# VectorE's frequency-domain sum written k1 by k1 into a tile of its own, one GpSimd sum behind it

## The chip, the cores and the metric

One core of one Trainium2 chip. The metric is the device time of one execution in microseconds, lower is better. The engines are named as in the profile: PE (TensorE matmul) and PEld (its weight load), DVE (VectorE), ACT (ScalarE), POOL (GpSimd) and SP (SyncE, which issues DMAs).

## The reference, cut to what matters

```python
u = x * v                                     # 4 batches, 11456 positions, 128 channels
h_filt = (np.maximum(pos_emb @ w1, 0) @ w2) * np.exp(-0.01 * pos)[:, None]
Uf = np.fft.rfft(u, n=2 * S, axis=1)
Hf = np.fft.rfft(h_filt, n=2 * S, axis=0)
y = np.fft.irfft(Uf * Hf[None], n=2 * S, axis=1)[:, :S]
attn = x * y
# then a mixture of experts on the 45824 rows of attn: top expert of 8 by
# logits = rows @ w_gate + modality_bias, out = gate * (relu(rows @ w1[e]) @ w2[e])
```

The change touches the product `Uf * Hf`, a complex multiplication for every batch, channel and frequency.

## The kernel before, in words

The convolution is a two-step transform by matmuls. The sequence is cut into N1 = 90 by N2 = 64; an outer transform over N1 turns positions n1 into k1, and a middle stage works on each k1: twiddle and transform over N2, multiply by the filter's spectrum, transform back. The kernel runs: filter, middle of batch 0, outer of batch 0 and 1, middle of batch 1, and so on, four middle stages in all; then the experts, which fill the second half of the execution. While a middle stage or outer stage of batch b runs, rows of batch b-1 are already sent to their expert's region by indirect DMAs that POOL issues (`send_rows`, L263).

A middle stage (`middle_stages`) walks over NG = 30 groups of G = 3 values of k1. Each group passes through stages that are shifted against each other by a table of steps (`MID`): in a step PE does, for four different groups, `turn` (six transposes to `aT`), `inverse` (twelve matmuls to `pw`), `back` (six transposes of the product to `yT`) and `spectrum` (twelve matmuls to `pz`). The order of PE, ACT, DVE and SP is the order of the program text, run step by step; each engine runs its own queue in order and waits for others by semaphores. POOL's order is that of the text too, with a `NoSync` dependency that puts one `send_rows` behind the second sum.

In `spectrum` of a group, `pz` in PSUM holds for both blocks (b) a real-like and an imaginary-like part (c) of 3 x 64 values with j, the k1 within the group, as the fastest index. The elementwise work on it is, in program order:

- L623 DVE twice: `more`[0], `more`[1] = parts of block 0 times a second filter row (128x384 each),
- L626: `more`[0] += `more`[1], on DVE for the first two groups of a stage (g < GD = 2), on POOL after that,
- L628 DVE twice: `part`[0], `part`[1] = all parts times the filter (128x768 each),
- L632 DVE: `part`[0] += `part`[1] (128x768, all of it in SBUF, in place),
- L633, on DVE or POOL like L626: block 1 of `part`[0] += `more`[0] (128x384),
- for g > 2 in batches 1 to 3, one L263 on POOL behind L633.

The result `part`[0] keeps j fastest, so `back` (L600 by way of the helper `turned`) transposes views with a step of three elements: `k["p"] = p.rearrange("p b c (k j) -> p b j (c k)", j=G)`. For block 0 the view is complete after L632, for block 1 after L633.

The tiles `aT`, `yT`, `part`, `more` and, in the outer stages, `seq`, `y` and `lT` come from one pool of NA = 11 buffers that are handed out in turn (`new_a`): a new tile waits until the tile that was handed out eleven requests ago has been read for the last time. `rings` holds the filter and twiddle constants, loaded ahead by SP.

Of the kernel before, what the change touches and what calls it, by code (L numbers as in the profile page):

```python
# [36 lines left out]
G = 3  # L37
# [139 lines left out]
def hyena_moe_kernel(ctx: ExitStack, tc: tile.TileContext, a: dict, out: bass.AP,  # L177
                     nb: int = B, nt: int = NF + NH):
    nc = tc.nc
    pe, act, dve, pool, sp = nc.tensor, nc.scalar, nc.vector, nc.gpsimd, nc.sync  # L180
# [13 lines left out]
    def bank(name):  # L194
        return banks[-1].tile([D, 512], F32, tag="ps", name=name)
# [30 lines left out]
    def ins_of(x):  # L226
        return getattr(x, "ins", x)
# [21 lines left out]
    def fetch(b):  # L249

        sp.dma_start(to_t[b % 2], xi[b].rearrange("(p c) -> p c", p=D))
        rows_back(b, 0)
        waiting.extend((b, c) for c in range(NR // D))

    def send_rows(n, behind=None, wait=None):


        for _ in range(min(n, len(waiting))):
            b, c = waiting.pop(0)
            if c % RC == 0:  # L260
                rows_back(b, c // RC + 1)
            ix, src = to_t[b % 2][:, c:c + 1], back_t[(b * NB + c // RC) % 3][:, c % RC]
            s = pool.indirect_dma_start(  # L263
                out=xs, out_offset=bass.IndirectOffsetOnAxis(ap=ix, axis=0), in_=src,
                in_offset=None, bounds_check=E * R - 1, oob_is_err=False)
            free_rows(scatters, s)
            if behind is not None:
                tc.add_manual_dep(ins_of(s), behind.name, order_dep, reason="order of issue")
            if wait is not None:
                tc.add_manual_dep(ins_of(s), wait.name, sync_dep, reason="pace")  # L270
# [83 lines left out]
    with ExitStack() as cv:  # L354
# [4 lines left out]
        GK = G * N2  # L359

        def pair(name):
            return pairs.tile([D, 2, 512], F32, tag="pp", name=name)

        def new_a(name, dt=F32):
            return st.tile([D, 1024], dt, tag="a", name=name, bufs=NA)
# [50 lines left out]
        def ring(name):  # L416
            r = ring_of[name]
            r[1] += 1
            return r[0][(r[1] - 1) % len(r[0])]
# [95 lines left out]
        def turn_back(g, blk, j):  # L515

            return A[:, blk, G * g + j].rearrange("p c n -> p (c n)")
# [53 lines left out]
        def middle_stages(b):  # L571

            kept = {}

            def load(g):
                k = kept[g] = {"b": ring("b")[0:2 * N2].rearrange("p (j d) -> p j d", j=G)}
                sp.dma_start(k["b"],
                             a["c_bc"][g, :, 0:2 * GK].rearrange("p (j d) -> p j d", j=G))
                h = k["h"] = ring("h").rearrange("p (m c k) -> p m c k", m=2, c=3)
                sp.dma_start(h[:, :, 1:3].rearrange("p m c k -> p m (c k)"),  # L580
                             hs[g].rearrange("p (m k) -> p m k", m=2))

            def minus(g):

                h = kept[g]["h"]
                act.mul(h[:, :, 0], h[:, :, 2], -1.0)

            def load_c(g):
                k = kept[g]
                k["c"] = ring("c")[0:2 * N2].rearrange("p (j d) -> p j d", j=G)  # L590
                sp.dma_start(k["c"],
                             a["c_bc"][g, :, 2 * GK:4 * GK].rearrange("p (j d) -> p j d", j=G))

            def turned(name, of):

                t = new_a(name)[0:2 * N2, 0:2 * G * D].rearrange("p (b m) -> p b m", b=2)
                for blk in range(2):
                    p = bank(name)
                    for j in range(G):
                        pe.transpose(p[0:2 * N2, D * j:D * j + D], of(blk, j), ident)  # L600
                    act.copy(t[:, blk], p[0:2 * N2, 0:G * D])
                return t

            def turn(g):
                kept[g]["aT"] = turned("aT", lambda blk, j: turn_back(g, blk, j))

            def spectrum(g):
                k = kept[g]
                pz = pair("pz")
                zv = pz[:, :, 0:2 * GK].rearrange("p b (m j) -> p b m j", j=G)  # L610
                for blk in range(2):
                    for j in range(G):
                        pe.matmul(zv[:, blk, :, j], k["aT"][:, blk, D * j:D * j + D],  # L613
                                  k["b"][:, j, :], start=True, stop=True)
                z = pz[:, :, 0:2 * GK].rearrange("p b (c m) -> p b c m", c=2)
                h = k["h"]


                part = [new_a("part")[:, 0:4 * GK].rearrange("p (b c m) -> p b c m", b=2, c=2)
                        for _ in range(2)]  # L620
                more = new_a("more")[:, 0:4 * GK].rearrange("p (b c m) -> p b c m", b=2, c=2)
                for i in range(2):
                    dve.tensor_mul(more[:, i], z[:, 0, i:i + 1].broadcast_to([D, 2, GK]),  # L623
                                   h[:, 1, 1 - i:3 - i])
                eng = dve if g < GD else pool
                eng.tensor_add(more[:, 0], more[:, 0], more[:, 1])  # L626
                for i in range(2):
                    dve.tensor_mul(  # L628
                        part[i], z[:, :, i:i + 1].broadcast_to([D, 2, 2, GK]),
                        h[:, 0:1, 1 - i:3 - i].broadcast_to([D, 2, 2, GK]))  # L630
                p = part[0]
                dve.tensor_add(p, p, part[1])  # L632
                added[0] = ins_of(eng.tensor_add(p[:, 1], p[:, 1], more[:, 0]))  # L633
                if g == GD and b > 0:
                    fetch(b - 1)
                if g > GD:
                    send_rows(1, added[0])
                k["p"] = p.rearrange("p b c (k j) -> p b j (c k)", j=G)

            def back(g):  # L640
                k = kept[g]
                k["yT"] = turned("yT", lambda blk, j: k["p"][:, blk, j])

            def inverse(g):
                k = kept.pop(g)
                for blk in range(2):
                    pw = bank("pw")
                    for j in range(G):
                        pe.matmul(pw[:, 2 * N2 * j:2 * N2 * (j + 1)],  # L649
                                  k["yT"][:, blk, D * j:D * j + D], k["c"][:, j, :],  # L650
                                  start=True, stop=True)
                    act.copy(A[:, blk, G * g:G * g + G].rearrange("p k c n -> p (k c n)"),
                             pw[:, 0:2 * GK])

            todo = dict(turn=turn, inverse=inverse, back=back, spectrum=spectrum, load_c=load_c,
                        load=load, minus=minus)
            return [(lambda g, n=n, t=int(t): g + t - (n == "back" and g >= NG - MB), todo[n])
                    for n, t in (w.split(":") for w in MID.split())]
# [234 lines left out]
        known, added = [], [None]  # L893
# [276 lines left out]
```

## Time and profile before

| | us |
|---|---|
| median of 3 runs (lowest, highest) | 2345.18 (2343.97, 2346.21) |
| the profiled execution | 2344.64 |
| its span, first to last instruction | 2342.9 |
| middle stage of batch 0, start of its first L632 to start of its last | 168.3 to 285.9 |
| middle stage of batch 1 | 440.1 to 566.2 |
| middle stage of batch 2 | 722.7 to 849.0 |
| middle stage of batch 3 | 1005.8 to 1131.4 |

The profiled execution lies 0.5 us below the median, so its trace can stand for the runs shown. The four middle stages together take about 500 us of the span; nothing of the change lies outside them. In a row of the timeline the first number is the start in us from the span's start, the second the duration in us; `x2` are two instructions that follow each other; a bracket at the end gives the idle time of the engine ahead and what ended it.

### The profile page before, as it was taken

How to read it: one execution, taken by the hardware profiler on the slowest of the kernel's cores; microseconds unless marked ns; L12 is line 12 of the kernel's file. 1: busy time of each engine (PE TensorE's matmuls, PEld its weight loads, DVE VectorE, ACT ScalarE, POOL GpSimd, SP SyncE). 2: the span in 40 equal slices, each digit the busy share in tenths (PEclk: the TensorE clock that was granted, in tenths of full speed). 3: DMA queues.
4: the chain of work that ended last, by engine and by line, in shares of the span. 5: the costliest groups of instructions: out<-in, count | busy, mean ns of one | idle time of the engine just before them, and what ended most of it. 6: DMA issues, size and time to landing. Idle time of an engine off the chain costs nothing. (4 is left out here: it accounts for less than half of the span.)

```text
span 2342.9 us, 42593 instructions
## 1 busy us (share of the span) xinstructions
PE 2248.1 (96%) x14058; PEld 1908.5 (81%) x14058; DVE 1876.0 (80%) x3197; ACT 1527.7 (65%) x2969; POOL 998.4 (43%) x987
## 2 busy tenths in 40 slices
PE   9899999899998999999997999999999999999998
PEld 8789977798777987689765888888888888888898
DVE  3789978798888978799687777777777877777797
ACT  5757667576665766667665666666666666666676
POOL 0305400276553765447662555455553333333333
PEclk9999999999999999999999999999999999999999
DMA  3976667567876678676575822222222111111111
GB/s 117 316 300 200 216 206 239 162 216 232 281 258 204 212 231 287 231 227 213 158 229 161 287 68 70 69 70 76 69 64 63 55 46 46 46 47 46 38 41 34
DMA packets 188745, 358.94 MB, mean 153 GB/s; under 512 B 33937, under 2 KB 120285, under 8 KB 188521
## 3 DMA queue, kind: packets, MB, share of 16 engines
q1 hardware_dynamic: 161753, 296.77, 39.8%
q0 software_dynamic: 26608, 59.36, 7.5%
q8 instruction: 114, 1.87, 0.3%
q14 instruction: 110, 0.90, 0.1%
q10 hardware_dynamic: 160, 0.03, 0.0%
HBM read 271.63 MB, written 84.83 MB: 152 GB/s over the span
## 5 line engine op out<-in xcount | busy, mean ns | idle before, releaser
L1053 DVE SCALAR_TENSOR_TENSOR hl<-ph,hh 128x512 fp32r<-128x512 f32 x724 | 499.0, 689 | 225.7 <-ACT hh L1052 216.8
L1052 ACT ACTIVATE hh<-ph 128x512 fp32r<-128x512 f32 x724 | 434.8, 601 | 360.2 <-PE ph L1049 351.2
L1089 POOL DMA_INDIRECT out<-ot,idx x362 | 357.5, 987 | 616.6 <-DVE ot L1086 534.0
L263 POOL DMA_INDIRECT xs<-back,to x360 | 378.4, 1051 | 212.9 <-DVE y L686 82.5
L1047 PE MATMUL ph<-xh,wh 128*128 128x512 f32 (+1 forms) x792 | 303.8, 384 | 1.8 <-ACT wh L1018 1.8
L1070 PE MATMUL po<-hh,wh 128*128 128x512 f32 (+1 forms) x792 | 302.7, 382 | 0.0
L1049 PE MATMUL ph<-xl,wh 128*128 128x512 f32 (+1 forms) x792 | 295.4, 373 | 0.0
L1072 PE MATMUL po<-hl,wh 128*128 128x512 f32 (+1 forms) x792 | 295.0, 372 | 0.1
L1048 PE MATMUL ph<-xh,wl 128*128 128x512 f32 (+1 forms) x792 | 294.4, 372 | 0.0
L1071 PE MATMUL po<-hh,wl 128*128 128x512 f32 (+1 forms) x792 | 293.8, 371 | 0.0
L626 POOL TENSOR_TENSOR more<-more 128x384 f32<-128x384 f32 x112 | 114.9, 1026 | 277.8 <-DVE more L623 222.8
L628 DVE TENSOR_TENSOR part<-pz,rings 128x768 f32<-128x768 f32 x240 | 216.9, 943 | 0.0
L613 PE MATMUL pz<-rings,aT 128*128 128x128 f32 x1440 | 185.9, 280 | 11.8 <-DMA rings<-in_c_bc 11.8
L649 PE MATMUL pw<-rings,yT 128*128 128x128 f32 x1440 | 187.7, 283 | 0.0
L613 PEld LDWEIGHTS pz<-rings,aT 128*128 128x128 f32 x1440 | 176.3, 197 | 12.4 <-issue 12.4
L633 POOL TENSOR_TENSOR part<-part,more 128x384 f32<-128x384 f32 x112 | 124.5, 1112 | 135.6 <-DVE part L632 117.1
L649 PEld LDWEIGHTS pw<-rings,yT 128*128 128x128 f32 x1440 | 178.1, 200 | 0.0
L464 PE MATMUL s<-fwd,seq 128*128 128x180 f32 x1024 | 168.1, 320 | 7.1 <-issue 4.4
L1049 PEld LDWEIGHTS ph<-xl,wh 128*128 128x128 f32 x792 | 149.4, 189 | 26.9
L1072 PEld LDWEIGHTS po<-hl,wh 128*128 128x128 f32 x792 | 149.1, 188 | 27.0 <-DVE hl L1053 0.5
L1047 PEld LDWEIGHTS ph<-xh,wh 128*128 128x128 f32 x792 | 149.7, 189 | 25.0 <-ACT wh L1018 2.2
L1048 PEld LDWEIGHTS ph<-xh,wl 128*128 128x128 f32 x792 | 149.9, 189 | 23.8 <-DVE wl L1019 0.4
(183 smaller groups left out, 4489.2 us busy)
## 6 DMA issues: line engine op xcount, KB each, us to landing
seq<-in_x SPq DMA_DIRECT2D x128, 512.0 KB, 5.1
rings<-in_c_bc SPq DMA_DIRECT2D x240, 192.0 KB, 3.4
rings<-hs SPq DMA_DIRECT2D x120, 384.0 KB, 3.5
seq<-in_v SPq DMA_DIRECT2D x64, 512.0 KB, 5.8
xr<-xo SPq DMA_DIRECT2D x64, 365.6 KB, 5.0
back<-xr SPq DMA_DIRECT2D x72, 325.0 KB, 3.7
x<-xs SPq DMA_DIRECT2D x82, 260.0 KB, 2.7
hs<-rings POOLq DMA_DIRECT2D x30, 384.0 KB
```

The lines of the kernel that those rows point to most:

```text
L263: s = pool.indirect_dma_start(out=xs, out_offset=bass.IndirectOffsetOnAxis(ap=ix, axis=0), in_=src, in_offset=None, bounds_check=E * R - 1 ...
L613: pe.matmul(zv[:, blk, :, j], k["aT"][:, blk, D * j:D * j + D], k["b"][:, j, :], start=True, stop=True)
L649: pe.matmul(pw[:, 2 * N2 * j:2 * N2 * (j + 1)], k["yT"][:, blk, D * j:D * j + D], k["c"][:, j, :], start=True, stop=True)
L1047: pe.matmul(p, k[0, "h"][:, f:f + D], k["xh"], start=True, stop=False)
L1048: pe.matmul(p, k[0, "l"][:, f:f + D], k["xh"], start=False, stop=False)
L1049: pe.matmul(p, k[0, "h"][:, f:f + D], k["xl"], start=False, stop=True)
L1052: act.activation(hh, ph, AF.Relu)
L1053: dve.scalar_tensor_tensor(hl, ph, 0.0, hh.bitcast(F32), op0=ALU.max, op1=ALU.subtract)
L1070: pe.matmul(po, k[1, "h"][:, f], hh[:, t], start=g == 0, stop=False)
L1071: pe.matmul(po, k[1, "l"][:, f], hh[:, t], start=False, stop=False)
L1072: pe.matmul(po, k[1, "h"][:, f], hl[:, t], start=False, stop=g == NCH - 1)
L1089: s = pool.indirect_dma_start(out=out, out_offset=bass.IndirectOffsetOnAxis(ap=k["idx"][:, j:j + 1], axis=0), in_=ot[:, j, :], in_offset=N ...
```

## The change

The sum L632 no longer goes back into `part`[0]. It goes into a new tile `p` from the same pool, in the layout that `back` now transposes: for every block, the 128 values (c and k) of each j side by side. The instruction reads both parts in the order in which they lie, j fastest, so successive results go to addresses 128 elements (512 bytes) apart: j = 0, 1, 2, then back and one element on. The second sum, now L635, adds into block 1 of `p`, which is contiguous, and reads `more`[0] through a view with a step of three elements. `back` transposes contiguous runs of 128. One more tile is requested from the pool per group, six in place of five.

```diff
-                p = part[0]
-                dve.tensor_add(p, p, part[1])
-                added[0] = ins_of(eng.tensor_add(p[:, 1], p[:, 1], more[:, 0]))
+                p = k["p"] = new_a("p")[:, 0:4 * GK].rearrange("p (b j m) -> p b j m", b=2, j=G)
+                dve.tensor_add(p.rearrange("p b j m -> p b m j"),
+                               part[0].rearrange("p b c (k j) -> p b (c k) j", j=G),
+                               part[1].rearrange("p b c (k j) -> p b (c k) j", j=G))
+                added[0] = ins_of(eng.tensor_add(
+                    p[:, 1], p[:, 1], more[:, 0].rearrange("p c (k j) -> p j (c k)", j=G)))
...
-                k["p"] = p.rearrange("p b c (k j) -> p b j (c k)", j=G)
```

Lines from L633 on stand two lines further down in the changed kernel: the second sum is L635, `inverse`'s matmul L651 and its copy L654; L632 keeps its number.

No instruction is added, removed or moved on any engine; what changes is the shape of two of them and what some wait for. On DVE, at the start of the first middle stage, where both sums of the first two groups run on DVE (`-` before, `+` after):

```order
 L626 TENSOR_TENSOR more<-more 128x384
 L628 TENSOR_TENSOR part<-pz,rings 128x768 x2
-L632 TENSOR_TENSOR part<-part 128x768
-L633 TENSOR_TENSOR part<-part,more 128x384
+L632 TENSOR_TENSOR p<-part 128x2x128x3
+L635 TENSOR_TENSOR p<-p,more 128x384
 L623 TENSOR_TENSOR more<-pz,rings 128x384 x2
```

The first sum is the same number of elements, now as 2 x 128 x 3 with the three as the fastest; the second writes `p`.

Further on in the same stage, where the second sums are POOL's, with the engines whose semaphores each instruction waits for. Before:

```order
L632 TENSOR_TENSOR part<-part 128x768 [waits DVE_49]
L623 TENSOR_TENSOR more<-pz,rings 128x384 [waits DMAHW0_49,PE_49]
L623 TENSOR_TENSOR more<-pz,rings 128x384 [waits Activation_49]
L628 TENSOR_TENSOR part<-pz,rings 128x768 [waits Pool_49]
L628 TENSOR_TENSOR part<-pz,rings 128x768
L632 TENSOR_TENSOR part<-part 128x768 [waits DVE_49]
```

And now:

```order
L632 TENSOR_TENSOR p<-part 128x2x128x3 [waits DVE_49]
L623 TENSOR_TENSOR more<-pz,rings 128x384 [waits DMAHW0_49,PE_49,Pool_49]
L623 TENSOR_TENSOR more<-pz,rings 128x384 [waits Activation_49]
L628 TENSOR_TENSOR part<-pz,rings 128x768 x2
L632 TENSOR_TENSOR p<-part 128x2x128x3 [waits DVE_49]
```

The wait for POOL, which is for a buffer of the pool that POOL wrote two steps earlier, has gone from the first L628 to the first L623 of a group, because the buffers fall to other tiles.

## The prediction

> **What bounds the kernel now.** I read the page's head first, then the busy time of the four stretches that hold the middle stages, because the change lies in them alone.
>
> ```profile
> span 2342.9 us, 42593 instructions
> PE 2248.1 (96%) x14058; PEld 1908.5 (81%) x14058; DVE 1876.0 (80%) x3197; ACT 1527.7 (65%) x2969; POOL 998.4 (43%) x987
> 168.00:288.00 120.00, 114.53 (x1005) 113.01 (x1005) 114.07 (x156) 84.58 (x195) 58.53 (x56) 1.00 0.62 199
> 440.00:568.00 128.00, 120.25 (x1021) 117.75 (x1022) 124.49 (x156) 87.17 (x199) 84.71 (x82) 0.99 0.72 230
> ```
>
> Over the whole span PE looks like the bound. In the stretches (columns: length, then PE, PEld, DVE, ACT, POOL busy) PE and DVE are level in batch 0 and DVE leads in batch 1, with POOL grown from 58.5 to 84.7 us. Two engines that close call for the timeline. First batch 0: DVE's rows, PE's rows, and the idle time in front of L623 over the whole stage.
>
> ```profile
> 250.13 0.96 DVE L632 TENSOR_TENSOR part<-part 128x768 f32<-128x768 f32 x1
> 251.37 1.02 DVE L623 TENSOR_TENSOR more<-pz,rings 128x384 f32<-128x384 f32 x2 [0.28 <-PE pz L613]
> 254.16 0.96 DVE L632 TENSOR_TENSOR part<-part 128x768 f32<-128x768 f32 x1
> ...
> 251.17 0.82 PE L600 MATMUL aT<-ident,A 128*128 128x128 f32 x6
> 253.16 0.85 PE L600 MATMUL yT<-ident,part 128*128 128x128 f32 x6
> 255.19 0.82 PE L600 MATMUL aT<-ident,A 128*128 128x128 f32 x6
> ...
> L623 DVE TENSOR_TENSOR more<-pz,rings 128x384 f32<-128x384 f32 x58 | 29.5, 551 | 4.6 <-PE pz L613 4.5
> L632 DVE TENSOR_TENSOR part<-part 128x768 f32<-128x768 f32 x30 | 28.7, 958 | 1.0
> ```
>
> A step takes 4.03 us (250.13 to 254.16), PE's own step is 4.02 (251.17 to 255.19) and DVE waits 0.28 us of it for `pz`: PE sets the pace, DVE is right behind, and its whole slack in the stage is 4.5 us. How fast DVE goes alone is seen at the start of batch 1, where no row is sent yet: 3.65 us a step.
>
> ```profile
> 451.61 0.96 DVE L632 TENSOR_TENSOR part<-part 128x768 f32<-128x768 f32 x1
> 455.26 0.96 DVE L632 TENSOR_TENSOR part<-part 128x768 f32<-128x768 f32 x1
> ```
>
> Then, in batches 1 to 3, the steps with a send. DVE's rows, POOL's rows, and the groups of the stretch 457 to 568:
>
> ```profile
> 545.39 1.47 DVE L632 TENSOR_TENSOR part<-part 128x768 f32<-128x768 f32 x1
> 549.55 1.48 DVE L632 TENSOR_TENSOR part<-part 128x768 f32<-128x768 f32 x1
> 553.73 1.47 DVE L632 TENSOR_TENSOR part<-part 128x768 f32<-128x768 f32 x1
> ...
> 545.00 1.04 POOL L626 TENSOR_TENSOR more<-more 128x384 f32<-128x384 f32 x1
> 547.01 1.01 POOL L633 TENSOR_TENSOR part<-part,more 128x384 f32<-128x384 f32 x1 [0.97 <-DVE part L632]
> 548.17 1.00 POOL L263 DMA_INDIRECT xs<-back,to  x1
> 549.18 1.03 POOL L626 TENSOR_TENSOR more<-more 128x384 f32<-128x384 f32 x1
> ...
> L632 DVE TENSOR_TENSOR part<-part 128x768 f32<-128x768 f32 x26 | 37.6, 1446 | 0.9
> L263 POOL DMA_INDIRECT xs<-back,to x26 | 26.0, 1000 | 4.0 <-issue 2.0 <-DVE more L623 0.2 <-DMA rings<-hs 0.2
> ```
>
> The same L632 takes 1446 ns here and 958 ns in batch 0. The rows show why: POOL's L626 runs from 549.18 to 550.21, L632 is issued inside it at 549.55 and ends at 551.03, 0.82 us after L626; 0.82 is about what 768 elements take. So L632 makes no progress until POOL's sum is done. That closes a ring: L632 ends at 546.86, 0.15 us later L633 starts (1.01), then 0.15, L263 (1.00), 0.01, L626 (1.03), and 0.82 for L632's own stream: 4.17 us, which is the distance of the L632 rows (549.55 to 553.73: 4.18). In 26 steps of each of the three later middle stages this ring sets the pace, neither PE nor DVE's own 3.65.
>
> **The change part by part.** The change lengthens or shortens links of exactly these paths.
>
> *L632 writes every result 512 bytes from the one before.* No row of before has 768 such writes, but smaller relatives exist:
>
> ```profile
> L808 DVE TENSOR_TENSOR ix<-sl,small x32: 185/186/203, 331.6 to 1280.6; 128x16 int32<-128x16 f32 x32
> L768 DVE TENSOR_TENSOR mb<-mb,small x32: 174/175/177, 319.0 to 1270.5; 128x16 f32<-128x16 f32 x32
> L758 DVE TENSOR_REDUCE mx<-lg x32: 365/371/377, 317.6 to 1269.0; 128x16 f32<-128x128 f32 x32
> L769 DVE TENSOR_TENSOR oh<-sco,mb x32: 291/292/293, 319.2 to 1270.7; 128x128 bf16<-128x128 f32 x32
> L302 DVE TENSOR_TENSOR scratch<-small,scratch x1: 628/628/628, 1166.8 to 1166.8; 1x480 f32<-1x480 f32 x1
> L305 DVE TENSOR_REDUCE scratch<-scratch x1: 1024/1024/1024, 1167.5 to 1167.5; 1x60 f32<-1x480 f32 x1
> ```
>
> L808 and L768 are the same addition of 16 elements, but L808 writes with a step of four elements: 186 against 175 ns, 0.69 ns an element. L758 reads 128 elements with a step of 16 and takes 79 ns more than L769, which reads as it lies: 0.62 ns an element. L305 reads 480 with a step of 60: 396 ns more than L302, 0.83 ns. All say that an access that hops at every element costs 0.62 to 0.83 ns on top of the roughly 1 ns of the element. The nearest, since it hops on the write side, is L808. I take 0.69 x 768 = 0.53 us, with ends 0.62 x 768 = 0.47 and 0.83 x 768 = 0.63; nothing would make the hop a gain. L632 then takes about 1.49 us unhindered, and ends about 1.35 us after L626 where it is blocked.
>
> The Trainium skill ("Vector Engine (DVE) Microarchitecture Reference", section 5.2 Measured stream behaviour on trn2) speaks more harshly of one form: a destination that steps by 24 words at every element ran at 2.50 ns per column against about 1.05 contiguous, while one that hops 4 KiB ran at 1.71. By the harsh figure L632 would gain 768 x 1.45 = 1.11 us and my sum would come to an estimated 2488 us; no row here shows such a price, and that case is a rival below.
>
> *The second sum reads `more` with a step of three.* No row shows POOL with a stepped read. Below it costs nothing; above I take the dearest hop of another engine, 0.83 x 384 = 0.32 us. As POOL takes 2.6 ns an element already (1.01 us for 384), part of a hop may hide; I take the middle, 0.16 us, with both ends kept.
>
> The Trainium skill ("GPSIMD Engine Reference", section 7 Performance pitfalls for Q7 kernels) puts a read with a step above 8 bytes at about 2.9 cycles an element in place of 1.9, which for 384 elements at its 1.2 GHz is an estimated 0.32 us; the step here is 12 bytes, and by it the sum below would be about 2431 us. No run here shows it yet.
>
> *`back` reads runs that lie side by side.* The weight loads of the stepped view are the longer ones now:
>
> ```profile
> L600 PEld LDWEIGHTS aT<-ident,A x720: 138/141/231, 162.0 to 1119.7; 128*128 128x128 f32 x180
> L600 PEld LDWEIGHTS yT<-ident,part x720: 188/198/231, 169.3 to 1134.3; 128*128 128x128 f32 x180
> ```
>
> They should fall from 198 to about 141 ns. But loads run beside matmuls: six `yT` transposes take 0.85 us against 0.82 for `aT`, so at most 0.03 us a step is on PE's path, and that only where PE sets the pace. After the longer L632 it no longer does in batch 0 (3.65 + 0.53 = 4.18 against 4.02), so I cost it at nothing; the cover is DVE's step, and without it the gain would be under 1 us in 30 steps.
>
> *One more tile from the pool of 11.* With six requests a step a buffer comes back after 11/6 steps in place of 11/5. `more` now takes the buffer of `p` from two steps earlier, whose last readers are the `yT` transposes that stand directly ahead of `pz` in PE's queue; L623 waits for that `pz` anyway, so the wait on POOL that moved to L623, with all of DVE's queue behind it, adds nothing. `p` takes the buffer of `aT`, read by the same `pz`. At the end of a stage SP's first `seq` loads may start later by part of a step; L450, which waits for them, is followed by 7.42 us of idle DVE:
>
> ```profile
> 287.10 2.05 DVE L450 TENSOR_TENSOR seq<-seq 128x1024 f32<-128x1024 f32 x1 [0.20 <-DMA seq<-in_v]
> 297.90 0.69 DVE L686 TENSOR_TENSOR y<-py,y 128x512 f32<-128x512 f32 x1 [7.42 <-ACT y L684]
> ```
>
> That hides a delay of several us; I cost it at nothing.
>
> *The sum.* Batch 0: 30 x 0.53 = 15.9, less the 4.5 us that DVE now waits for PE: 11.4. Each later stage: 26 steps of the ring gain 0.53 from L632 and 0.16 from L635, 17.9, and the four steps without a send, which run at DVE's own 3.65, gain 0.53 each, 2.1: 20.0, three times 60.2 (unrounded). The eight L635 that stay on DVE read with a step: 8 x 0.62 x 384 ns = 1.9. Together 73.5 us on the profiled execution's 2344.6, which is 0.5 below the median: 2418 us, slower by 3.1%. Once for all, 0.2% (4.7 us) is what I hold a measurement to tell from no change.
>
> **The rivals.** *POOL's sums change places with L632.* In the rows above L626 is issued 0.37 us ahead of L632 (549.18 and 549.55; 545.00 is the same 0.39 ahead of 545.39). A longer L635 pushes L626 back; from about 0.40 us on L632 is issued first and L626 waits for it. That POOL waits in its turn is seen where the bias operations, whose inputs are both in SBUF, come first:
>
> ```profile
> 501.98 1.18 DVE L632 TENSOR_TENSOR part<-part 128x768 f32<-128x768 f32 x1
> 503.09 1.21 DVE L709 TENSOR_TENSOR mb<-mf,bias 128x1024 f32<-128x1024 f32 x1
> 503.31 1.85 POOL L633 TENSOR_TENSOR part<-part,more 128x384 f32<-128x384 f32 x1 [0.97 <-DVE part L632]
> ```
>
> The ring would be cut and a step would be DVE's 3.65 + 0.53 = 4.18, as now. The order would hold, since POOL's 1.03 + 1.17 + 1.00 plus gaps fit in 4.18. Left would be batch 0's 11.4, the first four steps (2.1 a stage), some four steps a stage with bias operations, where L709 delays L632 and POOL is first again (0.53 + 0.40 each, 3.7) and the 1.9: about 31, 2376 us. Against it: my upper end for L635 is 0.32, under the point. For it: the margin is thin, and one late send would tip a step and those after it. Chance 0.20, runs that tip halfway included.
>
> *The hop is dear on the write side*, about twice L808's: L632 gains 1.06. Batch 0 gives 30 x 1.06 - 4.5 = 27.3, each later stage 26 x 1.22 + 4 x 1.06 = 36, with the 1.9 together 137: 2482 us. L808 speaks against it, with only 16 elements. The skill's 2.50 ns above would be this case. Chance 0.09.
>
> *The hop is free where it is written*, because DVE reads two streams and writes one. With L635 at +0.16 only 26 x 3 x 0.16 = 12.5 us are lost, 2357 us (0.05); with L635 under +0.05 the time is the same within 0.2% (0.04). And if in addition L635 gains over 0.40, the exchange above decides: L632 goes first at its old 0.96 us, the ring of 4.17 falls apart and PE's 4.02 sets the step, 0.15 x 22 x 3 = 9.9 us less, about 2335 us, faster (0.04).
>
> **How the numbers follow.** Forecast 0.58; its own range is 0.47 and 0 at the low end (30 x 0.47 - 4.5 + 90 x 0.47 = 51.9, 2397) and 0.63 and 0.32 at the high end (14.4 + 3 x 27.2 + 2 = 98, 2443). The range given reaches down over the exchange to the mild loss at 2357 and stops above at 2448; left out are the dear write, the faster case and no change, 0.17, and a little for what I have not seen. Slower 0.58 + 0.20 + 0.09 + 0.05 = 0.92, of which I give 0.01 to no change; same 0.05; faster 0.04.
>
> **What the changed profile would show.** Right: L632 near 1.49 us in batch 0 and near 2.2 us beside L626, ending about 1.35 us after it; steps of 4.2 us in batch 0 with no DVE idle for `pz`, and of 4.8 to 4.9 us with a send; `yT` weight loads at 141 ns; nothing changed after the last middle stage but a shift. L632 at 0.96 would refute the first term, L635 at 1.01 the second. L626 starting behind L632 would show the exchange; waits of L623 for POOL, or of L450 for `seq` far above 0.2 us, would show that the pool costs something after all.

## The result, and the profile after

The changed kernel takes 2413.1 us (median of 4 runs, 2412.6 to 2414.1) against 2345.1 us: a ratio of 1.029 (95% interval 1.0275 to 1.0305). 2418 was forecast. Its profiled execution took 2412.7 us. One execution of the changed kernel without its ring, further below, took 9040.9 us at a granted clock of 0.566 and is left out of that kernel's ratio. First the page's head, then the busy times of the stretches that hold the middle stages of batch 0 and batch 1 (length, then PE, PEld, DVE, ACT, POOL):

```profile
span 2410.9 us, 42519 instructions
PE 2268.9 (94%) x14058; PEld 1899.7 (79%) x14058; DVE 1949.4 (81%) x3197; ACT 1512.4 (63%) x2969; POOL 1009.7 (42%) x987
```

```profile
168.00:297.00 129.00, 118.10 (x1013) 111.57 (x1011) 127.83 (x157) 81.84 (x196) 59.62 (x55) 1.00 0.56 179
440.00:588.00 148.00, 125.64 (x1018) 115.89 (x1019) 142.41 (x171) 82.22 (x199) 80.91 (x75) 0.98 0.62 192
```

DVE is now busy for 127.8 of 129.0 us in batch 0: its slack is gone. In batch 1 it shows 142.4 of 148.0, but part of that is an L632 that stands still, as the rows below show. The changed instructions by source line (ns, lowest/median/highest), and DVE's groups of batch 0:

```profile
L632 DVE TENSOR_TENSOR p<-part x120: 1476/2227/2416, 170.0 to 1197.1; 128x768 f32<-128x768 f32 x120
L635 POOL TENSOR_TENSOR p<-p,more x112: 1090/1116/2067, 182.1 to 1199.4; 128x384 f32<-128x384 f32 x112
L635 DVE TENSOR_TENSOR p<-p,more x8: 683/692/708, 171.5 to 1061.5; 128x384 f32<-128x384 f32 x8
L600 PEld LDWEIGHTS yT<-ident,p x720: 137/141/231, 171.5 to 1200.9; 128*128 128x128 f32 x180
```

```profile
L632 DVE TENSOR_TENSOR p<-part 128x768 f32<-128x768 f32 x30 | 45.9, 1530 | 1.0
L623 DVE TENSOR_TENSOR more<-pz,rings 128x384 f32<-128x384 f32 x58 | 29.3, 546 | 0.0
```

Unhindered, L632 takes 1.53 us in place of 0.958. POOL's second sum takes 1.12 in place of 1.01. In this stage L623 waits for nothing any more. Now the timeline of a step in batch 0 and of a step with a send in batch 1, the latter with POOL's rows between DVE's:

```profile
209.35 1.54 DVE L632 TENSOR_TENSOR p<-part 128x768 f32<-128x768 f32 x1
213.51 1.55 DVE L632 TENSOR_TENSOR p<-part 128x768 f32<-128x768 f32 x1
214.90 1.01 DVE L623 TENSOR_TENSOR more<-pz,rings 128x384 f32<-128x384 f32 x2
...
576.80 2.25 DVE L632 TENSOR_TENSOR p<-part 128x768 f32<-128x768 f32 x1
579.23 1.12 POOL L635 TENSOR_TENSOR p<-p,more 128x384 f32<-128x384 f32 x1 [1.56 <-DVE p L632]
580.50 0.99 POOL L263 DMA_INDIRECT xs<-back,to  x1 [0.16 <-issue]
581.50 1.04 POOL L626 TENSOR_TENSOR more<-more 128x384 f32<-128x384 f32 x1
581.67 2.26 DVE L632 TENSOR_TENSOR p<-part 128x768 f32<-128x768 f32 x1
```

A step of batch 0 takes 4.16 us (209.35 to 213.51) and is DVE's own. A step with a send takes 4.87 (576.80 to 581.67), and the ring is still there: L632 is issued at 581.67 inside L626, which ends at 582.54, and itself ends at 583.93, 1.39 us later in place of 0.82. The middle stages, from the start of a stage's first L632 to the end of its last:

| stage | before | after | difference | forecast |
|---|---|---|---|---|
| batch 0 | 118.6 | 127.6 | +9.0 | +11.4 |
| batch 1 | 127.6 | 146.8 | +19.2 | +20.0 |
| batch 2 | 127.8 | 145.1 | +17.3 | +20.0 |
| batch 3 | 127.1 | 144.9 | +17.8 | +20.0 |

That is 63.3 of the 68.0 us by which the span grew. The other 4.7 lie outside the stages: 1.7 ahead of the first L632, 1.4 between stages, 1.7 behind the last (each rounded).

### The profile page after: what moved, and what is told of

It reads as the page before. It is cut to its first block, busy times and chain, and to the rows that moved or that the text cites. A ratio compares the mean times of both kernels' runs of the same rounds, so it can differ in the third digit from the quotient of the medians.

```text
span 2410.9 us, 42519 instructions
## 1 busy us (share of the span) xinstructions
PE 2268.9 (94%) x14058; PEld 1899.7 (79%) x14058; DVE 1949.4 (81%) x3197; ACT 1512.4 (63%) x2969; POOL 1009.7 (42%) x987
## 5 line engine op out<-in xcount | busy, mean ns | idle before, releaser
L632 DVE TENSOR_TENSOR p<-part 128x768 f32<-128x768 f32 x120 | 235.9, 1966 | 4.1
L626 POOL TENSOR_TENSOR more<-more 128x384 f32<-128x384 f32 x112 | 115.1, 1028 | 274.7 <-DVE more L623 215.4
L635 POOL TENSOR_TENSOR p<-p,more 128x384 f32<-128x384 f32 x112 | 135.7, 1212 | 194.6 <-DVE p L632 174.1
L628 DVE TENSOR_TENSOR part<-pz,rings 128x768 f32<-128x768 f32 x240 | 217.0, 944 | 0.0
L601 ACT COPY aT<-aT 128x384 f32<-128x384 f32 x240 | 103.5, 482 | 176.2 <-DVE p L632 123.3
L600 PE MATMUL yT<-ident,p 128*128 128x128 f32 x720 | 128.6, 293 | 76.3 <-POOL p L635 25.8
L651 PE MATMUL pw<-rings,yT 128*128 128x128 f32 x1440 | 185.6, 281 | 0.0
L651 PEld LDWEIGHTS pw<-rings,yT 128*128 128x128 f32 x1440 | 176.2, 198 | 0.0
```

Of the source, the lines that this page charges most:

```text
L651: pe.matmul(pw[:, 2 * N2 * j:2 * N2 * (j + 1)], k["yT"][:, blk, D * j:D * j + D], k["c"][:, j, :], start=True, stop=True)
```

## The experiments

The ratios below are to the kernel before on the same chip. Chips differ: on some the kernel before itself takes 2385 to 2388 us, and the kernels that ran there need 1247 to 1252 us behind the last middle stage in place of 1211. So totals are compared as ratios, and stages by their lengths.

**The extra tile alone.** The first sum goes to a new tile `p` but as the parts lie; the ring keeps its length.

```diff
-                p = part[0]
-                dve.tensor_add(p, p, part[1])
+                p = new_a("p")[:, 0:4 * GK].rearrange("p (b c m) -> p b c m", b=2, c=2)
+                dve.tensor_add(p, part[0], part[1])
```

> The kernel before, with one part of the change: L632 writes into a tile of its own, but in the order in which the parts lie, and nothing else is touched. Ring theory (the loss comes from L632's hopping writes and L635's stepped read): the time of before, 2345 us within 0.2%, L632 at 958 ns unhindered. Rival (the sixth tile a step from the pool of 11 makes engines wait, which the changed kernel's trace shows on ScalarE as 123 us of idle time ahead of aT): a good part of the 68 us, 2370 us or more.

Measured: 2349.3 us, ratio 1.0012 (1.0002 to 1.0021). DVE's rows of a step in batch 0 and one with a send:

```profile
212.27 0.96 DVE L632 TENSOR_TENSOR p<-part 128x768 f32<-128x768 f32 x1
216.29 0.96 DVE L632 TENSOR_TENSOR p<-part 128x768 f32<-128x768 f32 x1
...
546.98 1.51 DVE L632 TENSOR_TENSOR p<-part 128x768 f32<-128x768 f32 x1
551.18 1.49 DVE L632 TENSOR_TENSOR p<-part 128x768 f32<-128x768 f32 x1
```

A step takes 4.02 us in batch 0, and 4.20 in place of 4.17 with a send. A sixth tile costs 0.03 us a step and nothing more, so the loss is in the shapes of the two sums. Most of the 0.03 stands at one link: POOL's second sum starts 0.18 us behind L632's end in place of 0.16 (means of 48 ordinary steps); why is not shown.

**The second sum without its stepped read.** As the changed kernel, but L635 reads `more`[0] as it lies, so that it adds other elements.

```diff
-                    p[:, 1], p[:, 1], more[:, 0].rearrange("p c (k j) -> p j (c k)", j=G)))
+                    p[:, 1], p[:, 1], more[:, 0].rearrange("p c m -> p (c m)").rearrange("p (j m) -> p j m", j=G)))
```

> The changed kernel, with the second sum reading its second operand as it lies, without the step of three (so it adds other elements than it should). Ring theory: L635 on GpSimd falls from 1.11 to 1.00 us, and since it is a link of the ring every step with a send gets 0.11 us shorter, 78 x 0.11 = 8.6 us, with the eight sums on VectorE (692 to 558 ns, 1.1 us) about 2403.5 us. Rival (GpSimd's second sum has slack in the step): 2412 to 2413 us.

```profile
L635 POOL TENSOR_TENSOR p<-p,more x112: 992/1003/1818, 182.9 to 1190.8; 128x384 f32<-128x384 f32 x112
```

```profile
545.90 2.14 DVE L632 TENSOR_TENSOR p<-part 128x768 f32<-128x768 f32 x1
550.65 2.15 DVE L632 TENSOR_TENSOR p<-part 128x768 f32<-128x768 f32 x1
```

By source line L635 is back at 1.00 us; by the timeline the step is 4.75, 0.12 shorter. The stages took 127.2, 143.1, 144.3 and 142.3 us. Without its first step, whose length varies from run to run, each later stage is 3.0 to 3.1 us shorter than in the changed kernel, which is what the ring makes of 0.12 us in 26 steps. The total went the other way, 2438.2 us (ratio 1.039, 1.0376 to 1.0411) where 2403.5 was expected: behind the last middle stage 1245.9 us passed in place of 1211.6. With other values the experts' rows are routed otherwise, which would explain it but was not shown. The term is read from the stages, not from this total.

**The hop moved to the read side.** L632 writes `p` side by side and reads both parts with a step of three elements (12 bytes).

```diff
-                dve.tensor_add(p.rearrange("p b j m -> p b m j"),
-                               part[0].rearrange("p b c (k j) -> p b (c k) j", j=G),
-                               part[1].rearrange("p b c (k j) -> p b (c k) j", j=G))
+                dve.tensor_add(p, part[0].rearrange("p b c (k j) -> p b j (c k)", j=G),
+                               part[1].rearrange("p b c (k j) -> p b j (c k)", j=G))
```

> The changed kernel with the hop on the other side: L632 reads both parts with a step of three elements and writes p side by side in order. If a hop costs the same wherever it is: L632 near 1.5 us unhindered and 2405 to 2425 us. Rival (only hopping writes are dear, the two reads have a path each): L632 near 0.96 us, and only the longer L635 is left, 78 x 0.11 + 1, about 2355 us.

Measured: 2382.9 us, ratio 1.0162 (1.0143 to 1.018). DVE's rows in batch 0 and beside a send:

```profile
214.45 1.23 DVE L632 TENSOR_TENSOR p<-part 128x768 f32<-128x768 f32 x1
218.38 1.25 DVE L632 TENSOR_TENSOR p<-part 128x768 f32<-128x768 f32 x1
...
545.95 1.88 DVE L632 TENSOR_TENSOR p<-part 128x768 f32<-128x768 f32 x1
550.52 1.87 DVE L632 TENSOR_TENSOR p<-part 128x768 f32<-128x768 f32 x1
```

1.24 us unhindered: a step of 12 bytes on both reads costs 0.28 us, half of the write hop's 0.58. The step with a send is 4.57, and the ring's sum gives 4.17 + 0.28 + 0.11 = 4.56. So the same ring takes this price too. The total lies between the two that were expected.

**The kernel before without its ring.** The send is issued behind POOL's first sum (L626) in place of the second; all shapes as before.

```diff
-                eng.tensor_add(more[:, 0], more[:, 0], more[:, 1])
+                first = ins_of(eng.tensor_add(more[:, 0], more[:, 0], more[:, 1]))
+                if g > GD:
+                    send_rows(1, first)
...
-                if g > GD:
-                    send_rows(1, added[0])
```

> The kernel before, with each send moved from behind the second sum L633 to behind L626, so that GpSimd's L626 of the next group comes one send earlier and should be over when L632 starts. Ring theory: L632 falls to 0.96 us in all steps, the step with a send from 4.17 to the 4.02 us of TensorE, the twelve steps with bias operations from 5.02 to 4.79: 66 x 0.15 + 12 x 0.23 = 12.7 us less, 2332 us. Rival (the send, which now lies beside L632, holds VectorE up as L626 did, or the ring does not set the pace): 2345 us or more.

Measured: 2325.3 us, ratio 0.9905 (0.9886 to 0.9924). POOL's rows and DVE's first sum, here L634 (the second is L635), and that sum by source line:

```profile
537.16 1.00 POOL L635 TENSOR_TENSOR part<-part,more 128x384 f32<-128x384 f32 x1 [0.58 <-DVE part L634]
538.44 1.01 POOL L626 TENSOR_TENSOR more<-more 128x384 f32<-128x384 f32 x1 [0.29 <-DVE more L623]
539.61 1.00 POOL L263 DMA_INDIRECT xs<-back,to  x1 [0.16 <-issue]
540.06 0.96 DVE L634 TENSOR_TENSOR part<-part 128x768 f32<-128x768 f32 x1
```

```profile
L634 DVE TENSOR_TENSOR part<-part x120: 957/958/960, 171.4 to 1115.1; 128x768 f32<-128x768 f32 x120
```

DVE's sum now lies beside the send, not beside POOL's sum, and takes 0.96 us, like all 120 of them. The step is PE's 4.02, and the stages take 118.6, 119.9, 121.5 and 121.4 us. The gain is 20.7 us where 12.7 was expected, in part because some steps that the ring had held at 4.16 to 4.20 us fell below 4.02, to 3.65 to 3.75: the last of each stage and those just behind the bias operations. A second comparison of this kernel (below) gave the same.

> The kernel before with each send behind L626, a second time, beside the next run on one chip: 0.9905 of before, some 20 us less, by both theories.

Measured: 2325.9 us, ratio 0.9908 (0.9893 to 0.9923).

**The changed kernel without its ring.** The same move of the send, in the changed kernel.

> The changed kernel with the same move of the sends. Ring theory: L632 no longer meets L626, so a step with a send falls from 4.87 us to what VectorE needs alone, 4.15, and the twelve steps with bias operations from 5.60 to 5.28: 66 x 0.72 + 12 x 0.32 = 51 us less, 2362 us, 17 us above before. Rival (the hop costs by itself, the ring adds nothing to it): 2413 us less at most the 12.7 us that the move is worth without the change, 2400 us.

Measured: ratio 1.0067 (1.0041 to 1.0092).

```profile
539.40 1.00 POOL L263 DMA_INDIRECT xs<-back,to  x1 [0.15 <-issue]
539.59 1.54 DVE L634 TENSOR_TENSOR p<-part 128x768 f32<-128x768 f32 x1
543.74 1.52 DVE L634 TENSOR_TENSOR p<-part 128x768 f32<-128x768 f32 x1
```

The step is 4.15 us in all four stages (127.6, 128.1, 129.2, 128.8 us): DVE's own with a sum of 1.53. Nothing is left of POOL's longer sum, and the later stages lose about what batch 0 loses. Both experiments together show the ring: with it the change costs 0.70 us a step (4.17 to 4.87), without it 0.13 (4.02 to 4.15).

**Does L632 go first if it is issued first?** The forecast's rival put the point at about 0.40 us more on POOL. Three versions of the changed kernel delay POOL's first sum by useless fills of a spare tile: 480 elements between the send and the sum,

```diff
+                if g > GD + 1 and b > 0:
+                    idle = pool.memset(spare, 0.0)
...
                 first = eng.tensor_add(more[:, 0], more[:, 0], more[:, 1])
```

> The changed kernel with more work on GpSimd: a memset of 480 elements into a tile that nobody reads, about 0.3 us, between the send and L626 from the fifth group on in batches 1 to 3. Ring theory: L626 is issued 0.17 us ahead of L632 now, with the memset it comes behind; then L632 goes first and undisturbed at 1.54 us, L626 waits, and the step falls from 4.87 to 4.15 us in some 60 of 78 steps, 0.72 x 60 = 43 us less, about 2370 us, faster for added work. Rival (GpSimd's chain simply is too long, or the lock lets both go on slowly): 0.3 us a step more, 75 x 0.3, about 2436 us.

then the same fill ahead of the send, so that L632 is issued inside the send,

```diff
-                if g > GD:
-                    send_rows(1, added[0])
+                if g > GD and b > 0:
+                    idle = ins_of(pool.memset(spare, 0.0))
...
+                    send_rows(1, idle)
```

> The changed kernel with the same memset of 480 elements on GpSimd, about 0.53 us, but ahead of the send instead of behind it, so that at the time when L632 is issued GpSimd is inside the send, which did not hold the sum up where it lay beside it, and L626 is issued about 0.35 us behind L632. Exchange theory (whichever of the two sums is issued first goes first): L632 takes 1.54 us, L626 waits, the step with a send falls from 4.87 to 4.15 us outside the bias steps, and the middle stages of batches 1 to 3 end up near 130 us each in place of 145, some 45 us less than the changed kernel although GpSimd does more. Rival (VectorE loses to GpSimd whenever GpSimd has a sum to come, as the memset run suggests): the step grows to 4.87 + 0.53 = 5.4 us and the stages to 158 us.

and then two such fills.

> The changed kernel with two such memsets ahead of the send, about 1.0 us, so that L632 should be issued some 0.8 us before L626 starts, half of its own 1.54 us. Three theories of who waits. Order of issue with a wider margin than 0.27 us: L632 ends before or inside L626 at 1.54 us and the step is near 4.15 to 4.5 us. Pause (L632 runs, stops for L626, goes on): L632 ends about 0.7 us after L626 in place of 1.39, the step near 5.2 us. Port taken in advance (a GpSimd sum that is ready behind a running GpSimd instruction already keeps VectorE out): L632 still ends 1.39 us after L626, takes about 3.2 us, and the step is 5.8 us.

The first and the second lost alike: ratios 1.0421 (1.0389 to 1.0453) and 1.0433 (1.0417 to 1.0449), later stages of 157 to 158 us. Rows of the first (DVE's sum is L638 there, POOL's L630), and then of the second (L633 and L627):

```profile
580.54 0.52 POOL L628 MEMSET spare<- 128x480 f32 x1
580.72 2.69 DVE L638 TENSOR_TENSOR p<-part 128x768 f32<-128x768 f32 x1
581.00 1.02 POOL L630 TENSOR_TENSOR more<-more 128x384 f32<-128x384 f32 x1
```

```profile
581.31 0.99 POOL L263 DMA_INDIRECT xs<-back,to  x1 [0.16 <-issue]
582.04 2.69 DVE L633 TENSOR_TENSOR p<-part 128x768 f32<-128x768 f32 x1
582.31 1.03 POOL L627 TENSOR_TENSOR more<-more 128x384 f32<-128x384 f32 x1
```

In both DVE's sum starts 0.27 to 0.28 us ahead of POOL's, inside a fill or a send, and still ends 1.39 us behind it, with nothing gained by its head start. The step is 5.30. So the exchange as the forecast described it doesn't happen.

The third shows that there is such a point, only further out: ratio 1.028 (1.0215 to 1.0345), stages 145.3, 145.8 and 144.8. Its timeline, in three places of batch 1 (a step with bias operations, one after them, an ordinary one):

```profile
514.03 1.00 POOL L263 DMA_INDIRECT xs<-back,to  x1 [0.25 <-issue]
514.37 3.07 DVE L633 TENSOR_TENSOR p<-part 128x768 f32<-128x768 f32 x1
515.05 1.02 POOL L627 TENSOR_TENSOR more<-more 128x384 f32<-128x384 f32 x1
...
540.12 1.55 DVE L633 TENSOR_TENSOR p<-part 128x768 f32<-128x768 f32 x1
541.02 1.38 POOL L627 TENSOR_TENSOR more<-more 128x384 f32<-128x384 f32 x1
...
581.65 1.55 DVE L633 TENSOR_TENSOR p<-part 128x768 f32<-128x768 f32 x1
582.63 1.31 POOL L263 DMA_INDIRECT xs<-back,to  x1 [0.25 <-issue]
583.96 1.03 POOL L627 TENSOR_TENSOR more<-more 128x384 f32<-128x384 f32 x1
```

With a lead of 0.68 us DVE still yields (3.07 us, ending 1.37 behind POOL's sum). With 0.90 it goes first, and now POOL's sum takes 1.38 in place of 1.02. In the ordinary step the lead has grown to 2.31 us and the two don't meet at all. The twelve leads of 0.51 to 0.68 us in this kernel all yield and the five of 0.90 to 1.05 all go first. But the twelve all lie in steps with bias operations and the five in other steps; there the longest lead that yields is 0.42 us, in the second kernel. So in an ordinary step the point is shown only to lie between 0.42 and 0.90 us. The ordinary step is now POOL's own, 4.56 or 4.79 us with the length of the send (1.02 + 1.12 + 0.51 + 0.50 + 1.07 to 1.31, and gaps), above the 4.15 to 4.5 expected. POOL carries two fills, 1.01 us, more a step than in the changed kernel and the stages are no longer for it (144.8 to 145.8, against 144.9 to 146.8). What of POOL's queue decides early that its next sum will have the input is open; no run here shows it.

The Trainium skill ("SBUF — State Buffer", section Who interferes with whom) says that issue order decides which of the two blocks. The trace agrees in the bias steps quoted in the prediction, where POOL was idle and L709, 0.22 us ahead, made it wait, and so did every lead of 0.04 to 0.34 us over an idle POOL in the traces of before, of the changed kernel and of the kernel before with its send moved; it doesn't agree where POOL's sum stands directly behind another POOL instruction: there leads up to 0.68 us were lost.

**A layout that needs no hop.** `pz` is written with k side by side for each j (in the filter's own stage too), the first sum is two sums of 384 whose reads and writes are runs of 64, `back` reads runs of 128; the send stands behind L626.

```diff
-                zv = pz[:, :, 0:2 * GK].rearrange("p b (m j) -> p b m j", j=G)
+                zv = pz[:, :, 0:2 * GK].rearrange("p b (c j k) -> p b j c k", c=2, j=G)
...
+                for blk in range(2):
+                    dve.tensor_add(runs[:, blk], lies(part[0][:, blk]), lies(part[1][:, blk]))
```

> The goal of the layout without hops, with the sends moved: the matmuls to pz write each j's 64 values of a part side by side, so the elementwise work reads as it lies in another order of columns; L632 becomes two sums of 384 elements that write runs of 64 into p; the second sum reads and writes runs of 64; back transposes contiguous runs. If runs of 64 cost nothing: L632 at 0.48 us twice, yT weight loads at 141 ns, TensorE's step 4.02 less up to 0.03 us, 2329 to 2333 us. Rival (the two sums in place of one cost 0.1 us a step more on VectorE and the pattern with runs is slow): VectorE's step above 4.02 and 2335 us or more.

> The layout without hops with the sends moved, on one chip with the run before. If TensorE's step of 3.99 us in place of 4.02 counts: 1 to 3 us less than the run before. If the two sums' 0.08 us more on VectorE count in the steps with bias operations as much: the same within 0.1%.

Measured: ratio 0.9942 (0.992 to 0.9964), and 0.9932 (0.9918 to 0.9945) on the chip on which the kernel before with its send moved had 0.9908. DVE's sums and PE's rows:

```profile
540.59 1.03 DVE L637 TENSOR_TENSOR p<-part 128x384 f32<-128x384 f32 x2
541.79 1.02 DVE L623 TENSOR_TENSOR more<-pz,rings 128x384 f32<-128x384 f32 x2 [0.18 <-issue]
...
539.54 0.82 PE L600 MATMUL yT<-ident,p 128*128 128x128 f32 x6
543.53 0.82 PE L600 MATMUL yT<-ident,p 128*128 128x128 f32 x6
```

The two sums take 1.03 us together, the transposes fall from 0.85 to 0.82 and the step from 4.02 to 3.99, as it had to where PE sets the pace. The total shows no gain from it: the stages are as long (119.4, 120.5, 121.6, 121.6 on the second chip). Of what ran, the kernel before with its send moved has the lowest ratio, though its interval and that of this layout touch.

## Why the prediction was right, point by point

*What bounds the kernel.* Shown. Taking the ring away (both moves of the send) took the 4.17 and the 4.87 us out of the later stages, and each change of a link by 0.11, 0.28 or 0.58 us appeared in the step with nearly that size.

*The write hop, 0.53 us a sum.* Measured 0.58 at the median (1.534 in batch 0 against 0.958) and 0.52 at the lowest (1476 against 957 ns). L808's 0.69 ns an element was the right relative: 0.75 at the median. Of the Trainium skill's two figures in the section cited, the 2.50 ns of the 24-word step is far from it; the hop over 4 KiB, 1.71 against 1.05, gives an estimated 0.51 us, and the trace agrees with 0.52 to 0.58. The *dear write* and the *free hop* are refuted by the same rows.

*Blocked behind L626.* Forecast 1.35 us behind it, measured 1.39 at the median (1.35 to 1.43).

*The stepped read on POOL, 0.16 us.* Measured 0.11, between the ends. The Trainium skill's rule ("GPSIMD Engine Reference", section 7) would have given an estimated 0.32; only one of the sum's two inputs is stepped here, and whether that is why is not shown. The eight L635 on DVE gained 0.13 us each (558 to 692 ns), not 0.24: together they cost 1.1 us, not 1.9.

*The sum by stages.* Ordinary steps with a send gained 0.70 us each where 0.69 was forecast. That it is so close is luck: L632's end behind L626 moved by 0.57 us, not 0.53, and L635 grew by 0.11, not 0.16, and the two errors cancel; the other 0.02 is the later start of L635 that the extra tile alone showed. In and around the bias operations, five steps a stage, the gain was about 0.6.

The stages together came out 10 us under the forecast. In the steps that DVE sets by itself the step grew by 0.49 (3.65 to 4.14), not 0.53, although the sum grew by 0.58: the next L623 now starts 0.16 us ahead of the sum's recorded end (214.90 against 215.06), and before it started 0.09 ahead (452.48 against 452.57):

```profile
452.48 1.01 DVE L623 TENSOR_TENSOR more<-pz,rings 128x384 f32<-128x384 f32 x2
```

Batch 0 gained 9.0 in place of 11.4, because DVE's slack was also larger than the 4.5 us of idle time that were subtracted: a step at PE's 4.02 lies 0.37 above DVE's own 3.65, of which the idle row shows 0.28. The largest part, about 5 us, is the first step of each later stage (from the end of its first L632 to the end of its second), which the forecast had grow by 0.53: it fell by 0.24, 1.78 and 1.58 us, since there DVE waits for PE's second `pz`. DVE's row of batch 2 before, and after:

```profile
726.85 1.02 DVE L623 TENSOR_TENSOR more<-pz,rings 128x384 f32<-128x384 f32 x2 [2.62 <-PE pz L613]
```

```profile
756.05 1.02 DVE L623 TENSOR_TENSOR more<-pz,rings 128x384 f32<-128x384 f32 x2
```

The wait of 2.62 us is gone. That it is the change's doing is not shown: over all kernels run here this first step lies anywhere between 5.6 and 8.0 us. The 4.7 us outside the stages were not forecast either and are of the same kind; the first L632 starts anywhere from 168.3 to 172.1 us in these traces, ahead of all that was edited. So the total is nearer to the forecast (4.9 us) than the stages are (10), and that too is luck.

*The pool.* The cost of nothing held (0.03 us a step by the experiment), the reasoning did not. The buffers are not handed out strictly in turn: in the changed kernel as built, `more` takes the buffer of `more` from two groups earlier, last read by L635, `p` takes that of `part`[1], and `aT` that of `part`[0], which L632 still reads. L623 never sat idle for POOL (its idle time in the whole trace is 18.3 us, all for `pz`), but the wait of `aT` was overlooked. In the page's groups of after:

```profile
L601 ACT COPY aT<-aT 128x384 f32<-128x384 f32 x240 | 103.5, 482 | 176.2 <-DVE p L632 123.3
```

ACT waits 123.3 us for L632, against 4.5 before. It has the time: the extra-tile kernel has 48.9 us of this wait and lost 0.03 us a step. L450 waits 1.80 us for `seq` behind batch 0 (0.20 before) and is followed by 7.58 us of idle DVE: hidden, as costed.

*The exchange, chance 0.20.* It didn't occur, but the argument against it was too weak. L626 did move towards L632, from 0.37 to 0.16 us ahead (means of 48 ordinary steps), twice as far as the 0.11 of L635 alone, since DVE's queue closes up behind L632 too; yet even with L632 0.28 us ahead nothing changed. Where L632 does go first, from somewhere between 0.42 and 0.90 us of lead in an ordinary step, the fills that brought it there had made POOL's own step 4.56 to 4.79 us.

## What to carry to other kernels

Where two engines use one resource in a cycle, walk the ring of waits first: every nanosecond on a link counts in full, and the first edit to try is the order that opens the ring, which here gave 1% where a new layout inside the ring lost 3%. Price a hop by the nearest row with a hop, per element, and check the cover on the engine that is second by a few per cent, because it becomes the bound at once. Shorter weight loads (198 to 141 ns) are worth at most 0.03 us a step where they lie beside matmuls.

## What the runs showed of the hardware

- Writes 512 bytes apart (three, then back and one element on) cost DVE 0.68 to 0.75 ns an element (768 elements: 957 to 1476, median 1534 ns); a step of 12 bytes on both reads 0.36 (median 1238 ns); runs of 64 none that shows (384 elements in 0.55 us).
- A DVE sum of two SBUF operands beside POOL's issue of an indirect DMA isn't held: 957 to 960 ns for all 120 sums with the send moved. Beside POOL's sum it is.
- Issued 0.23 to 0.68 us ahead of a POOL sum that stands directly behind another POOL instruction, it yields all the same, to the sum's end; from 0.90 us on it is POOL that waits (1.38 in place of 1.02 us). Ahead of an idle POOL a lead of 0.04 us was enough.
